# Raw inputs loaded from ScalarE's queue behind its rounding, and features-B sums in two buffers

## The chip, the cores and the metric

The kernel runs on one core of a Trainium2 chip. A core has a matmul engine (TensorE, PE in the profile; its weight loads are PEld), a vector engine (VectorE, DVE), a scalar engine (ScalarE, ACT), a general engine (GpSimd, POOL), a sync engine that here only issues DMAs (SyncE, SP), and 16 DMA engines that carry what any engine issues. Each engine works through its own instructions in order and waits on semaphores. The metric is the device time of one execution in microseconds, lower is better.

## The reference

Two stages over 8 x 4096 = 32768 tokens with 192 features:

```python
# 1: a causal convolution with 7 taps, softmax of the taps per head
w = exp(weight - max); w = w / (sum(w) + 1e-9)          # 8 heads of 24 features
out[b, s, h] = sum_k w[h, k] * x_pad[b, s + k, h]       # 6 zeros ahead of each sequence
# 2: an MLP with a squared relu
h = x @ w_in                 # 192 -> 2048
r = maximum(h, 0)
g = s * (r * r) + b
return g @ w_out             # 2048 -> 192
```

All data are float32.

## The kernel before, in words

**Tiles.** The 192 features are split into features A (the first 128) and features B (the last 64). Tokens are handled in 32 groups n of 1024, each of two blocks j of 512 tokens. The 2048 hidden features are eight pairs p of 256. Features A of a group are one raw tile `xA` (128 x 1030, with six columns of the tokens before), features B of both blocks are stacked in one raw tile `xB` (128 x 518). Both come from the pool `xin` (line 102), which has one buffer of each, so a group's raw tile can be loaded only when the convolution of the group before has read it.

**Convolution.** DVE makes it with seven instructions (taps) a piece (`Tokens.conv`, lines 180 and 182). A group has three pieces: B, A0 and A1. A piece `acc` is then split in a high and a low half for the matmuls (`Tokens.split`): ACT rounds it (L214), DVE subtracts the rounded part (L207), and two DMAs on SP copy the halves crosswise (`swap`, L190 and L191).

**A step.** For n, j, p the function `first` makes 18 matmuls into one of two PSUM tiles `h` (L527). ACT takes the relu (L555), which frees that `h`, and the square (L563). DVE rounds it (`qh`, L565) and subtracts (`ql`, L569). Two steps later `second` multiplies by the output weights for features A (12 matmuls, L700). After the eighth pair ACT evicts two accumulators (L707, L708), POOL adds them (L709) and SP stores the sum (L710).

**A batch.** The squares are kept in a ring of twelve tiles (line 97), and every 24 steps `batch` makes the features-B sums of three blocks in a row: for each block 64 small matmuls as the trace counts them (`second_B`, L719), some pieces of convolution, and `evict_B`:

```python
nc.scalar.activation(o, accs[0], AF.Identity, scale=sb, bias=bias[:, 1:2])   # L729, o is oB
nc.scalar.activation(o2, accs[1], AF.Identity, scale=sb)                     # L730, o2 is oB2
nc.gpsimd.tensor_tensor(o, o, o2, op=ALU.add)                                # L731
nc.sync.dma_start(oC, o[DB:P])                                               # L732
nc.gpsimd.tensor_tensor(oC, oC, o[0:DB], op=ALU.add)                         # L733
nc.sync.dma_start(outT[P:D, t0 : t0 + BLK], oC)                              # L734
```

The buffers oA, oB, oC, oB2 and oA2 are five parts of one tile `outs` (line 99, places in line 590), one of each.

**What sets the order.** The whole program is unrolled. `in_order` (line 944) keeps the instructions of DVE, ACT and PE in the order in which the code makes them, DMAs that one of them issues included. SP's and POOL's order behind the start is chosen by the compiler's scheduler from its own estimate of when each instruction can go. The convolution is a generator (`pieces`, line 770): `step` and `batch` draw a given number of parts from it with `convolve`. One part is one tap, one rounding, or one subtraction with its swap. A rounding is held back (`gate`) until a set step, while the taps of the next piece may run ahead. Between the last tap and the gate the code issues the next group's raw loads (lines 779 to 784): xB behind piece B, xA behind piece A1, on SP, and only ordered behind the last DMA of the start (`headed`). For every fourth group, which begins a sequence, POOL also clears the first six columns (L166). Lines 168 and 172 are the two loads.

Of the kernel before, what the change touches and what calls it, by code (L numbers as in the profile page):

```python
# [9 lines left out]
F32 = mybir.dt.float32  # L10
# [7 lines left out]
P = 128  # L18
BLK = 512
# [28 lines left out]
def conv_attention_then_squared_relu_mlp(  # L48
# [23 lines left out]
    nc = tc.nc  # L72
# [3 lines left out]
    PAD = K - 1  # L76
    DB = D - P
    NF = 2 * NPAIR
    SUP = 2 * BLK
    NSUP = T // SUP  # L80
# [15 lines left out]
    xs = ctx.enter_context(tc.tile_pool(name="xs", bufs=2))  # L96
    act = ctx.enter_context(tc.tile_pool(name="act", bufs=RING))
    wide_w = ctx.enter_context(tc.tile_pool(name="wide_w", bufs=1))
    outs = wide_w.tile([P, 5, BLK], F32, name="outs")
    W = wide_w.tile([P, NPAIR, 2, CB], F32R, name="W")  # L100
    WB = wide_w.tile([P, NPAIR, 2, DB], F32, name="WB")
    xin = ctx.enter_context(tc.tile_pool(name="xin", bufs=1))
# [5 lines left out]
    def last_of(*engines):  # L108


        traced = nc.cur_bb.bb.instructions
        last = [next(i for i in reversed(traced) if i.engine == e.engine) for e in engines]

        @contextmanager
        def context():
            with ExitStack() as stack:
                for i in last:
                    stack.enter_context(tc.issue_after(i))
                yield

        return context
# [23 lines left out]
    class Tokens:  # L145
# [3 lines left out]

        def load(self):  # L150
            n = self.n
            if n == 0:
                self.load_B()
                self.load_A(PAD + BLK)
                fetch(0, 0, CI)
                nc.sync.dma_start(self.xA[:, PAD + BLK :], xA[:, BLK:SUP])
            else:
                self.load_B()
                self.load_A(PAD + SUP)

        def load_A(self, cut):
            t0 = self.n * SUP
            self.xA = xin.tile([P, PAD + SUP], F32, name="xA")
            skip = PAD if t0 % seq == 0 else 0
            if skip:
                nc.gpsimd.memset(self.xA[:, 0:PAD], 0.0)  # L166
            x0 = t0 - PAD
            nc.sync.dma_start(self.xA[:, skip:cut], xA[:, x0 + skip : x0 + cut])

        def load_B(self):  # L170
            self.xB = xin.tile([P, PAD + BLK], F32, name="xB")
            nc.sync.dma_start(self.xB, xB[self.n])

        def conv(self, acc, x, w, width):

# [161 lines left out]
    def fetch(p, a=0, z=None):  # L337
        if a == 0:
            words[p] = places[p % 3][:, 0 : 2 * CT].rearrange("p (f w) -> p f w", w=2)
        z = z or CT  # L340
        nc.sync.dma_start(
            words[p][:, a:z].rearrange("p f w -> p (f w)"), w_words[p, :, 2 * a : 2 * z]
        )
# [19 lines left out]
    tok = {0: Tokens(0)}  # L363
# [224 lines left out]
        return w_outA(1, f, r)  # L588

    room = {"oA": 0, "oB": 1, "oC": 2, "oB2": 3, "oA2": 4}  # L590

    def out_tile(name):
        return outs[:, room[name], :]

    held = {}

# [10 lines left out]
    def second_whole(n, j, p, qh, ql):  # L607
# [17 lines left out]
        if p == NPAIR - 1:  # L625
            t0 = n * SUP + j * BLK
            oA, oB = (hold(n, j, k) for k in range(2))
            oB = oB[0:DB]
            nc.scalar.activation(oA, a1, AF.Identity, scale=sb)
            oC = out_tile("oC")[0:DB]  # L630
            nc.scalar.activation(oC, a2[DB:P, :], AF.Identity, scale=sb[DB:P])
            nc.vector.scalar_tensor_tensor(
                oB, a2[0:DB, :], sb[0:DB], oC, op0=ALU.mult, op1=ALU.add
            )
            unbiased.append((oA, outT[0:P, t0 : t0 + BLK], 0))
            unbiased.append((oB, outT[P:D, t0 : t0 + BLK], 2))
            del acc[n, j]

    def second_split(n, j, p, qh, ql):
# [19 lines left out]
        if p == NPAIR - 1:  # L659
            t0 = n * SUP + j * BLK  # L660
            early = (n, j) == (1, 0)

            o = {k: hold(n, j, k) for k in range(2)}
            for k, name in ((1, "oB"), (0, "oA")):
                o[k + 2] = out_tile(name + "2")
                nc.scalar.activation(
                    o[k], accs[k], AF.Identity, scale=sb, bias=0.0 if early else bias[:, k : k + 1]
                )
                nc.scalar.activation(o[k + 2], accs[k + 2], AF.Identity, scale=sb)
            nc.gpsimd.tensor_tensor(o[1], o[1], o[3], op=ALU.add)  # L670

            oC = out_tile("oC")[0:DB]
            nc.sync.dma_start(oC, o[1][DB:P])
            nc.gpsimd.tensor_tensor(o[0], o[0], o[2], op=ALU.add)
            toA, toB = outT[0:P, t0 : t0 + BLK], outT[P:D, t0 : t0 + BLK]
            oB = o[1][0:DB] if early else oC
            if not early:
                nc.sync.dma_start(toA, o[0])
            nc.gpsimd.tensor_tensor(oB, oC, o[1][0:DB], op=ALU.add)
            if early:  # L680
                unbiased.extend(((o[0], toA, 0), (oB, toB, 2)))
            else:
                nc.sync.dma_start(toB, oB)
            del acc[n, j]
# [81 lines left out]
    queue = []  # L766
# [3 lines left out]
    def pieces():  # L770

        def whole(n, kind, j):
            t = tok.setdefault(n, Tokens(n))
            acc = xs.tile([P, BLK], F32, name="acc")
            x = t.xB if kind == "B" else t.xA[:, j * BLK :]
            for k, _ in enumerate(t.conv(acc, x, tapB if kind == "B" else tapA, BLK)):
                if k < K - 1:
                    yield None
            with headed():
                if kind == "B" and n + 1 < NSUP:  # L780
                    tok[n + 1] = Tokens(n + 1)
                    tok[n + 1].load_B()
                elif j == 1 and n + 1 < NSUP:
                    tok[n + 1].load_A(PAD + SUP)
            yield "tapped"
            gate = 16 * n - (0 if j else 8 if kind == "A" else 16)
            while n + j > 1 and now[0] < gate:
                yield "gated"
            once = (n, kind) == (1, "B")
            split = t.split_B_at_once(acc) if once else t.split(kind, j, acc)  # L790
            next(split)
            yield "after" if once else "cast"
            next(split)
            ready.add((n, kind, j))
            yield None

        order = [(1, "A", 0), (1, "B", 0), (1, "A", 1)]
        for n in range(2, NSUP):
            order += [(n, "B", 0), (n, "A", 0), (n, "A", 1)]
        todo = [whole(*c) for c in order]  # L800
        ahead = False
        while todo:
            said = next(todo[0], "over")
            if said == "over":
                todo.pop(0)
                ahead = False
                continue
            if said in ("cast", "gated") and len(todo) > 1 and not ahead:
                if said == "cast":
                    yield said  # L810
                said = next(todo[1])
                ahead = said == "tapped"
            yield said
# [130 lines left out]
    with in_order(nc.vector, nc.scalar, nc.tensor):  # L944
        with in_order(nc.sync):
            head()
        headed = last_of(nc.sync)
# [58 lines left out]
```

## Time and profile before

| | |
|---|---|
| Median of 3 runs | 2259.8 us (2258.36 to 2260.03) |
| The profiled execution | 2259.81 us, its span 2258.0 us |
| Granted TensorE clock | 0.998 |
| Busy: PE, DVE, ACT, POOL | 99%, 71%, 59%, 12% of the span |
| DMA queue of SP (q1) | 114.50 MB, 18.3% of 16 engines |
| DMA queue of ACT (q10) | 0.13 MB, 0.0% |

The profile is of one execution. Its span runs from the first to the last instruction; the device time of the same execution is 1.8 us longer. A row of a timeline has the start in the span, the length (both in microseconds), the engine, the line of the kernel, the operation, what it writes and reads, how many instructions are merged in the row, and, in brackets, how long the engine stood idle before it and what ended that wait. A row of the waits has who waited for whom, the total, the number of times and the longest. A row for one line of code has the durations in nanoseconds (least, median, most). SPq and ACTq are the sequencers, which issue DMAs.

### The profile page before, as it was taken

How to read it: one execution, taken by the hardware profiler on the slowest of the kernel's cores; microseconds unless marked ns; L12 is line 12 of the kernel's file. 1: busy time of each engine (PE TensorE's matmuls, PEld its weight loads, DVE VectorE, ACT ScalarE, POOL GpSimd, SP SyncE). 2: the span in 40 equal slices, each digit the busy share in tenths (PEclk: the TensorE clock that was granted, in tenths of full speed). 3: DMA queues.
4: the chain of work that ended last, by engine and by line, in shares of the span. 5: the costliest groups of instructions: out<-in, count | busy, mean ns of one | idle time of the engine just before them, and what ended most of it. 6: DMA issues, size and time to landing. Idle time of an engine off the chain costs nothing.

```text
span 2258.0 us, 44538 instructions
## 1 busy us (share of the span) xinstructions
PE 2229.2 (99%) x19334; PEld 1616.9 (72%) x19334; DVE 1601.9 (71%) x1859; ACT 1323.9 (59%) x1449; POOL 274.7 (12%) x199
## 2 busy tenths in 40 slices
PE   9999999999999999999999999999999999999999
PEld 6788686868677676768686767767686858686775
DVE  8888677767776676767677767775776767677753
ACT  8758464646555464746465656556474646465654
POOL 0011101010101111110101010101111010102011
PEclk9999999999999999999999999999999999999999
DMA  5112212121211112121211211111212121112110
GB/s 164 38 37 82 62 34 62 43 52 49 55 53 53 45 45 60 41 62 39 56 38 53 57 52 48 52 55 41 59 36 62 34 62 43 53 40 59 48 36 22
DMA packets 46004, 117.48 MB, mean 52 GB/s; under 512 B 7728, under 2 KB 7984, under 8 KB 45808
## 3 DMA queue, kind: packets, MB, share of 16 engines
q1 hardware_dynamic: 45664, 114.50, 18.3%
q8 instruction: 151, 2.47, 0.5%
q14 instruction: 45, 0.37, 0.1%
q10 hardware_dynamic: 144, 0.13, 0.0%
HBM read 31.64 MB, written 25.17 MB: 25 GB/s over the span
## 4 chain that ended last, share of the span: by engine, by line
PE 77%; DVE 7%; ACT 6%; DMA 5%; POOL 3%; issue 2%; SPq 0%; DVEq 0%; POOLq 0%; ACTq 0%
PE h L527 42%; PE acc L700 27%; PE acc L719 4%; DMA outs<-outs 4%; DVE acc L182 4%; ACT q L563 2%; ACT q L555 2%; POOL outs L733 2%; DVE ql L569 2%; PE acc L646 2%; DVE qh L565 1%; ACT outs L730 1%; POOL outs L731 1%; PE h L719 1%; PE acc L256 1%
## 5 line engine op out<-in xcount | busy, mean ns | idle before, releaser
L555 ACT ACTIVATE q<-h 128x1024 f32<-128x1024 f32 x512 | 525.0, 1025 | 437.2 <-PE h L527 428.1
L565 DVE CAST qh<-q 128x1024 fp32r<-128x1024 f32 x482 | 334.9, 695 | 486.5 <-ACT q L563 484.8
L569 DVE TENSOR_TENSOR ql<-q,qh 128x1024 fp32r<-128x1024 f32 x498 | 613.9, 1233 | 55.9 <-ACT qh L565 4.9
L700 PE MATMUL acc<-qh,W 64*128 64x512 f32 x3816 | 591.6, 387 | 0.0
L563 ACT ACTIVATE q<-q 128x1024 f32<-128x1024 f32 x512 | 543.4, 1061 | 16.1
L527 PE MATMUL h<-sA,W 64*128 64x512 f32 x3024 | 431.1, 390 | 17.4 <-ACT q L555 17.4
L527 PE MATMUL h<-wB,W 64*128 64x512 f32 x1536 | 431.6, 387 | 0.0
L527 PE MATMUL h<-sB,W 64*128 64x512 f32 x1536 | 431.6, 387 | 0.0
L527 PE MATMUL h<-wA,W 64*128 64x512 f32 x3024 | 428.5, 387 | 0.6 <-DMA wA<-sA 0.6
L700 PEld LDWEIGHTS acc<-qh,W 64*128 64x128 f32 x3816 | 362.1, 184 | 73.2 <-issue 0.8
L719 PE MATMUL acc<-q,WB 64*64 64x512 f32 x3712 | 402.9, 590 | 0.0
L700 PE MATMUL acc<-ql,W 64*128 64x512 f32 x1908 | 378.6, 390 | 5.6 <-DVE ql L569 5.6
L527 PEld LDWEIGHTS h<-sA,W 64*128 64x128 f32 x3024 | 282.4, 184 | 95.4 <-ACT q L555 23.4
L182 DVE SCALAR_TENSOR_TENSOR acc<-xA,tap,acc 128x512 f32<-128x512 f32 x378 | 326.4, 864 | 6.8
L527 PEld LDWEIGHTS h<-wA,W 64*128 64x128 f32 x3024 | 286.6, 185 | 60.0 <-DMA wA<-sA 1.4
L719 PEld LDWEIGHTS acc<-q,WB 64*64 64x64 f32 x3712 | 140.0, 133 | 252.3 <-issue 252.3
L527 PEld LDWEIGHTS h<-wB,W 64*128 64x128 f32 x1536 | 283.1, 184 | 30.4
L527 PEld LDWEIGHTS h<-sB,W 64*128 64x128 f32 x1536 | 283.1, 184 | 30.2 <-issue 0.2
L709 POOL TENSOR_TENSOR outs<-outs 128x512 f32<-128x512 f32 x59 | 99.6, 1688 | 1293.8 <-ACT outs L708 1293.8
L729 ACT ACTIVATE outs<-acc,bias,sb 128x512 f32<-128x512 f32 x58 | 45.2, 779 | 325.8 <-POOL outs L733 294.5
L700 PEld LDWEIGHTS acc<-ql,W 64*128 64x128 f32 x1908 | 182.0, 184 | 53.0 <-DVE ql L569 17.6
L182 DVE SCALAR_TENSOR_TENSOR acc<-xB,tap,acc 128x512 f32<-128x512 f32 x186 | 167.0, 898 | 3.6
(145 smaller groups left out, 879.1 us busy)
## 6 DMA issues: line engine op xcount, KB each, us to landing
wA<-sA SPq DMA_DIRECT2D x124, 256.0 KB, 3.7
wB<-sB SPq DMA_DIRECT2D x62, 256.0 KB, 3.5
outT<-outs SPq DMA_DIRECT2D x59, 256.0 KB, 2.0
xA<-in_xA SPq DMA_DIRECT2D x24, 515.0 KB, 3.7
xB<-in_xB SPq DMA_DIRECT2D x32, 259.0 KB, 2.8
outT<-outs SPq DMA_DIRECT2D x62, 128.0 KB, 2.3
outs<-outs SPq DMA_DIRECT2D x59, 128.0 KB, 2.2
q<-in_w SPq DMA_DIRECT2D x7, 768.0 KB, 4.6
```

What stands on the lines that cost most here:

```text
L182: nc.vector.scalar_tensor_tensor(acc, src, w[:, k : k + 1], acc, op0=ALU.mult, op1=ALU.add)
L527: nc.tensor.matmul(h[:, i, :], w_in(w, p, chunk[0], rows), chunk[part], start=start, stop=stop)
L555: nc.scalar.activation(q, h, AF.Relu)
L563: nc.scalar.activation(q, q, AF.Square)
L565: cast(qh, q)
L569: nc.vector.tensor_tensor(ql, q, qh.bitcast(F32), op=ALU.subtract)
L646: nc.tensor.matmul(accs[to + 2 * i][0:cols], w(f, r), q[r, f % 2, :], start=start and f == 0, stop=stop and f == NF - 1,)
L700: nc.tensor.matmul(accs[i], w(f, r), q[r, f % 2, :], start=f == 0 and lo == 0, stop=f == ends[i] and lo == 2,)
L709: nc.gpsimd.tensor_tensor(o, o, o2, op=ALU.add)
L719: nc.tensor.matmul(accs[r.start // HB][i * DB : (i + 1) * DB], WB[r, p, i, :], q[r, i, :], start=p == 0, stop=p == NPAIR - 1, skip_group_c ...
L729: nc.scalar.activation(o, accs[0], AF.Identity, scale=sb, bias=bias[:, 1:2])
L733: nc.gpsimd.tensor_tensor(oC, oC, o[0:DB], op=ALU.add)
```

## The change

Three things are changed. The raw loads of groups 2 to 31 move from SP's queue to ACT's, and from behind the last tap to behind the rounding L214 of the same piece. They lose the order that `headed` gave them and stand in ACT's fixed order instead; the POOL memset of the six columns is written in the code at the new place too. The loads of groups 0 and 1 stay on SP. The sums of features B get a second buffer: `outs` has six parts, and each call for oB takes the part that the call before did not take (parts 1 and 5). That is 2 KB more for each partition.

```diff
-    outs = wide_w.tile([P, 5, BLK], F32, name="outs")
+    outs = wide_w.tile([P, 6, BLK], F32, name="outs")
...
-        def load_A(self, cut):
+        def load_A(self, queue, cut=PAD + SUP):
...
-            nc.sync.dma_start(self.xA[:, skip:cut], xA[:, x0 + skip : x0 + cut])
+            queue.dma_start(self.xA[:, skip:cut], xA[:, x0 + skip : x0 + cut])
...
-            nc.sync.dma_start(self.xB, xB[self.n])
+            queue.dma_start(self.xB, xB[self.n])
...
     room = {"oA": 0, "oB": 1, "oC": 2, "oB2": 3, "oA2": 4}
+    turn = [0]

     def out_tile(name):
-        return outs[:, room[name], :]
+        k = room[name]
+        if name == "oB":
+            turn[0] = 1 - turn[0]
+            k += 4 * turn[0]
+        return outs[:, k, :]
...
-            with headed():
-                if kind == "B" and n + 1 < NSUP:
-                    tok[n + 1] = Tokens(n + 1)
-                    tok[n + 1].load_B()
-                elif j == 1 and n + 1 < NSUP:
-                    tok[n + 1].load_A(PAD + SUP)
             yield "tapped"
             gate = 16 * n - (0 if j else 8 if kind == "A" else 16)
             while n + j > 1 and now[0] < gate:
...
             split = t.split_B_at_once(acc) if once else t.split(kind, j, acc)
             next(split)
+            if kind == "B" and n + 1 < NSUP:
+                tok[n + 1] = Tokens(n + 1)
+                tok[n + 1].load_B(nc.scalar)
+            elif j == 1 and n + 1 < NSUP:
+                tok[n + 1].load_A(nc.scalar)
             yield "after" if once else "cast"
```

More of the change, by code (lines that the diff above doesn't have):

```diff
@@ L151, in load @@
             n = self.n
-            if n == 0:
-                self.load_B()
-                self.load_A(PAD + BLK)
+            self.load_B(nc.sync)
+            if n:
+                self.load_A(nc.sync)
+            else:
+                self.load_A(nc.sync, PAD + BLK)
                 fetch(0, 0, CI)
                 nc.sync.dma_start(self.xA[:, PAD + BLK :], xA[:, BLK:SUP])
-            else:
-                self.load_B()
-                self.load_A(PAD + SUP)
-        def load_A(self, cut):
+        def load_A(self, queue, cut=PAD + SUP):
             t0 = self.n * SUP
@@ L167, in load_A, with load_B @@
             x0 = t0 - PAD
-            nc.sync.dma_start(self.xA[:, skip:cut], xA[:, x0 + skip : x0 + cut])
-        def load_B(self):
+            queue.dma_start(self.xA[:, skip:cut], xA[:, x0 + skip : x0 + cut])
+        def load_B(self, queue):
             self.xB = xin.tile([P, PAD + BLK], F32, name="xB")
-            nc.sync.dma_start(self.xB, xB[self.n])
+            queue.dma_start(self.xB, xB[self.n])
         def conv(self, acc, x, w, width):
```

## The prediction

> **What bounds the kernel now.** I read the busy table first, then the waits of the matmul engine (PE), then the timelines of each engine around the places where PE stood still. The busy table says that PE is the engine to follow:
>
> ```profile
> PE 2229.2 (99%) x19334; PEld 1616.9 (72%) x19334; DVE 1601.9 (71%) x1859; ACT 1323.9 (59%) x1449; POOL 274.7 (12%) x199
> ```
>
> So nothing counts that does not close a hole in PE. The waits of PE (total us, times, longest) name nearly all of its holes:
>
> ```profile
> PE h L527 <- ACT q L555: 17.4, 10, 2.2
> PE acc L700 <- DVE ql L569: 5.6, 16, 0.4
> ...
> PE h L527 <- DMA wA<-sA: 0.6, 1, 0.6
> ```
>
> The 26 of the first two rows all lie just behind a batch, the stretch in which PE makes the features-B sums of three blocks (L719). Nineteen batches come 24 steps apart; the one at 2134 comes when the last raw input has long been loaded. Its PE timeline is the measure for the others (start, length):
>
> ```profile
> 246.31 1.95 PE L719 MATMUL acc<-q,WB 64*64 64x512 f32 x16
> ...
> 2130.59 0.84 PE L527 MATMUL h<-sA,W 64*128 64x512 f32 x6
> ...
> 2134.08 0.66 PE L719 MATMUL acc<-q,WB 64*64 64x512 f32 x4
> ...
> 2154.84 0.98 PE L527 MATMUL h<-sA,W 64*128 64x512 f32 x6
> ...
> 2158.42 0.84 PE L527 MATMUL h<-sA,W 64*128 64x512 f32 x6
> ...
> 2161.82 0.84 PE L527 MATMUL h<-sA,W 64*128 64x512 f32 x6
> ```
>
> A step without a stall is 2161.82 - 2158.42 = 3.40 us. A batch is 2154.84 - 2134.08 = 20.76, the step behind it 3.58, the step before it 3.49. Between two batches lie 24 steps, so a period without loss is 20.76 + 3.58 + 22 x 3.40 + 3.49 = 102.63 us. The first batch starts at 246.31 and the nineteenth at 2134.08: 18 periods took 1887.77 us instead of 1847.3. **PE loses 40.4 us there**, 2.2 a period. That is more than the 23 us of waits, since a matmul that restarts also follows at a wider distance.
>
> Batches alternate between two kinds. In the first kind both waits of PE are seen (batch at 1504):
>
> ```profile
> 1524.98 0.98 PE L527 MATMUL h<-sA,W 64*128 64x512 f32 x6
> ...
> 1528.56 0.84 PE L527 MATMUL h<-sA,W 64*128 64x512 f32 x6
> ...
> 1534.27 0.96 PE L527 MATMUL h<-sA,W 64*128 64x512 f32 x6 [2.15 <-ACT q L555]
> ...
> 1538.46 0.85 PE L527 MATMUL h<-sA,W 64*128 64x512 f32 x6
> ...
> 1542.10 0.85 PE L527 MATMUL h<-sA,W 64*128 64x512 f32 x6
> ```
>
> Against 3.40 the last three steps shown take 5.71, 4.19 and 3.64: 3.34 us lost, 2.31 of it in the first. ScalarE (ACT) shows why:
>
> ```profile
> 1511.36 0.78 ACT L729 ACTIVATE outs<-acc,bias,sb 128x512 f32<-128x512 f32 x1 [0.49 <-PE acc L719]
> 1512.03 0.68 ACT L730 ACTIVATE outs<-acc,sb 128x512 f32<-128x512 f32 x1
> 1524.98 0.78 ACT L729 ACTIVATE outs<-acc,bias,sb 128x512 f32<-128x512 f32 x1 [12.26 <-POOL outs L733]
> ...
> 1531.95 0.78 ACT L729 ACTIVATE outs<-acc,bias,sb 128x512 f32<-128x512 f32 x1 [5.62 <-POOL outs L733]
> ...
> 1533.20 1.02 ACT L555 ACTIVATE q<-h 128x1024 f32<-128x1024 f32 x1
> ```
>
> The second and third evictions want to write the one buffer oB, which POOL's last add of the block before (L733) still reads; the relu (L555) that gives PE its next h buffer stands behind them. L733 in turn waits for the copy L732, and SP could not issue that:
>
> ```profile
> 1519.06 0.34 SPq L168 DMA_DIRECT2D xA<-in_xA  x1
> 1519.49 0.46 SPq L732 DMA_DIRECT2D outs<-outs  x1
> ```
>
> POOL and VectorE (DVE) say what each of the two had waited for:
>
> ```profile
> 1512.86 1.68 POOL L731 TENSOR_TENSOR outs<-outs 128x512 f32<-128x512 f32 x1 [5.77 <-ACT outs L730]
> ...
> 1523.68 1.26 POOL L733 TENSOR_TENSOR outs<-outs 64x512 f32<-64x512 f32 x1 [9.14 <-DMA outs<-outs]
> ```
>
> ```profile
> 1513.33 5.70 DVE L182 SCALAR_TENSOR_TENSOR acc<-xA,tap,acc 128x512 f32<-128x512 f32 x6
> ```
>
> The copy's data stood from 1512.86 + 1.68 = 1514.54. The raw load L168 is ahead of it in SP's order and waits for the last tap at 1519.03. The copy is 4.9 us late for a load that nobody needs yet.
>
> In the second kind (batch at 1400) an xB load does the same, with a shorter delay; PE then only lacks the low halves:
>
> ```profile
> 1414.23 0.34 SPq L172 DMA_DIRECT2D xB<-in_xB  x1
> 1414.67 0.47 SPq L732 DMA_DIRECT2D outs<-outs  x1
> ```
>
> ```profile
> 1421.28 0.98 PE L527 MATMUL h<-sA,W 64*128 64x512 f32 x6
> ...
> 1431.45 0.50 PE L700 MATMUL acc<-ql,W 64*128 64x512 f32 x2 [0.34 <-DVE ql L569]
> ```
>
> ```profile
> 1427.22 1.02 ACT L555 ACTIVATE q<-h 128x1024 f32<-128x1024 f32 x1
> ```
>
> The batch at 2134 has one oB buffer too, but no load ahead of the copy:
>
> ```profile
> 2150.04 0.78 ACT L729 ACTIVATE outs<-acc,bias,sb 128x512 f32<-128x512 f32 x1 [7.47 <-POOL outs L733]
> ...
> 2157.75 1.02 ACT L555 ACTIVATE q<-h 128x1024 f32<-128x1024 f32 x1
> ```
>
> Counted from the first h behind the batch, the relu starts 1533.20 - 1524.98 = 8.2 us late in the first kind, 1427.22 - 1421.28 = 5.9 in the second and 2157.75 - 2154.84 = 2.9 here, where nothing is lost. So the bound in this stage is the time of that relu: 2.9 costs nothing, 5.9 costs the low-half stall, 8.2 costs both.
>
> **The change, part by part.** *The copy is freed.* No load stands ahead of L732 on SP, so it goes as in the batch at 2134. There L733 was done, and let the second eviction go, at 2150.04, 15.96 us after the batch's start. The batch at 1504 starts at 1524.98 - 20.76 = 1504.22, so its first L733 is done near 1520.2 instead of 1524.9.
>
> *Two buffers.* The second eviction writes the other oB and needs only its sum. The three sums are ready 6.92 us apart (20.76 / 3), at about 1511.1, 1518.1 and 1525.0. The second goes at 1518.3; the third, which shares its oB with the first, finds it free since 1520.2 and goes at 1525.2. With its partner it takes 0.78 + 0.68, to about 1526.6. The relu then waits for h alone: 2.5 us behind the first h, earlier than the harmless 2.9. The low halves follow it by about 4.2 us (relu, square, cast, subtraction), so the 16 waits on ql go too. What is late next is nothing on PE; oC stays single, but POOL and SP alone wait for it, and oB2 is free when L731 is done, some 4 us ahead of each next use. The larger outs moves the tiles behind it by 2 KB a partition. No row shows such a shift; it could only lengthen or shorten instructions off PE's way, with the cover that the next part finds.
>
> *The loads on ACT.* Sixty loads (two for each of 30 groups) leave SP and stand on ACT directly behind the rounding L214. What they wait for, DVE's last tap, the rounding has already waited for, so no new wait is added; the cost is the issue. The trace has one DMA issued by ACT, and SP's own for the same load, with its time to landing:
>
> ```profile
> L764 ACTq DMA_DIRECT2D outT<-outs x1: 371/371/371, 2254.6 to 2254.6; - x1
> ```
>
> ```profile
> L168 SPq DMA_DIRECT2D xA<-in_xA x32: 333/346/431, 1.7 to 2090.1; - x32
> ...
> DMA to landing us min/median/max: 3.4/3.7/5.7
> ```
>
> So about 0.37 us each, 22 us of ACT in all. Queued behind are the next relu and square, and through them DVE's cast and PE. By the order that the code sets, which repeats every 48 steps with six loads, four of six fall into ordinary steps. Such a step on ACT, DVE and PE:
>
> ```profile
> 1553.19 0.60 ACT L214 CAST sA<-acc 128x512 fp32r<-128x512 f32 x1
> 1554.56 1.03 ACT L555 ACTIVATE q<-h 128x1024 f32<-128x1024 f32 x1 [0.77 <-PE h L527]
> ```
>
> ```profile
> 1557.51 1.23 DVE L569 TENSOR_TENSOR ql<-q,qh 128x1024 fp32r<-128x1024 f32 x1
> ...
> 1565.46 0.48 DVE L180 TENSOR_SCALAR acc<-xA,tap 128x512 f32<-128x512 f32 x1
> ```
>
> ```profile
> 1561.61 0.39 PE L700 MATMUL acc<-ql,W 64*128 64x512 f32 x2
> ```
>
> ACT idles 0.77 us behind the rounding, which hides 0.37. Were it not enough, the low half is ready at 1558.74 and used at 1561.61, 2.87 us later. So a load may hold ACT for 0.77 + 2.87 = 3.64 us before PE notices. Between an issue of 0.37 and one that lasts to the landing, 5.7 at most, I take the first, the only row of ACT itself, and so a price of nothing. The other two loads fall behind roundings inside or just ahead of a batch, where PE has 20.76 us of its own work.
>
> *Later loads.* They now wait for the rounding, which the code holds back to a set step. The tightest is the xA load behind the rounding at 1553.19: its first reader is the L180 at 1565.46, 11.7 us after the rounding ends, against a landing of 3.7, at most 5.7. Hidden by 6 us or more. The memset of the first columns moves on POOL with the load and only waits less.
>
> *Sum.* Of the 40.4 us I leave 2 (the wait for a swap, third row of the waits above, and some 0.08 a batch): 38.4 us go. The profiled execution took 2259.81 us with a span of 2258.0; the median of the three runs is 2259.8, so one scale serves both. 2259.8 - 38.4 = 2221.4 us.
>
> **The rivals.** *Only half of it:* the relu's stall goes, but the low halves stay late, because DVE, SP's new order or the third eviction still holds the relu to about 5 us. For it: the batch at 1400 shows the ql stall without any PE wait on ACT. Against it: at 2.9 us it is gone, and I find 2.5. What goes are ten waits of 1.74 on average, each with 0.16 of wider spacing (2.31 - 2.15): 19.0 us. Time 2241.
>
> *No change:* the queue is not what matters, and the loads only move their issue. Sixty times 0.35 us, 21 us, leave SP, none of it on PE's way: 2259.8. Beside this stands the Trainium skill, "DMA: Bandwidth & Descriptors", section "Issuing engines are not separate DMA queues": issuing from several engines saves only the time on the sequencer that it takes to initiate the DMA, usually small. By that rule as it stands the time would be 2259.8. Here the copy was late by the 4.9 us in which the load stood first in SP's order, waiting, and that speaks against the rule as a full account.
>
> *Slower:* a load holds ACT until some transfer in flight on SP's queue has landed, for instance over a shared completion count. Its place are the 40 loads in ordinary steps; beyond 3.64 us each further microsecond costs PE 40 us. It decides from 3.64 + 38.4 / 40 = 4.6 us a load. Held for the longest landing above, with the issue, 0.35 + 5.7 = 6.05, that is 40 x 2.41 = 96 us lost and 38.4 won: 2317. At the median landing, 4.05, it would be 16 lost: 2238, still faster. Against it: SP itself issued L732 0.43 us after L168, without awaiting its landing.
>
> **How the numbers follow.** A measurement of this kernel can tell about 0.2% (4.5 us) from no change. The forecast has 0.77, half of it 0.14, no change 0.04, slower 0.05. The likeliest time is 2221.4. If all 40.4 us go it is 2219.4; the lower end, 2217, adds some 2 us for the steps ahead of the first batch, which the periods don't count. The upper end takes in the half case, 2241. Faster by over 0.2% is 0.77 + 0.14 = 0.91, within 0.2% 0.04, slower 0.05.
>
> **What would show it.** Right: L729 waits for PE's sums and no longer for L733; L732 follows L731 within some tenths; the relu starts about 2.5 us behind the first h; the two waits of PE shrink to near nothing; batches stand 102.7 us apart. Wrong: ACT idle behind a DMA issue, L180 waiting for xA or xB, or ql waits that remain behind the batches.

## The result, and the profile after

The changed kernel takes 2220.59 us (median of four runs, 2220.06 to 2221.55); the kernel before, beside it, 2259.91 us. The ratio is 0.983 (95% interval 0.981 to 0.984). Faster was forecast, with 2221.4 us.

The change moves the lines: L729, L731, L732 and L733 of before are now L733, L735, L736 and L737; L527, L555 and L719 are L526, L554 and L723. First the busy table of the page and the waits of PE:

```profile
PE 2213.0 (100%) x19334; PEld 1617.7 (73%) x19334; DVE 1638.0 (74%) x1859; ACT 1329.0 (60%) x1449; POOL 287.1 (13%) x199
```

```profile
PE acc L391 <- POOL xA L165: 1.0, 1, 1.0
PE h L526 <- DMA wA<-sA: 0.3, 1, 0.3
PE acc L620 <- DVE ql L568: 0.2, 1, 0.2
```

The 26 waits behind the batches (17.4 and 5.6 us) are gone; what is left is a single wait for a swap and two near the start. PE's timeline has the first and the nineteenth batch:

```profile
246.00 1.52 PE L723 MATMUL acc<-q,WB 64*64 64x512 f32 x12
...
2094.80 2.38 PE L723 MATMUL acc<-q,WB 64*64 64x512 f32 x20
```

18 periods now take 1848.8 us, 102.71 each; without loss they would take 1847.3. The loss of 40.4 us has become 1.5. The 18 periods are shorter by 1887.77 - 1848.80 = 39.0 us, of the 39.5 us by which the span became shorter (2258.0 to 2218.5).

The batch that was at 1504 is now at 1478.6. ACT, POOL and SP in it ("issue" stands for time in which the engine waited for nothing that the profile shows):

```profile
1492.57 0.78 ACT L733 ACTIVATE outs<-acc,bias,sb 128x512 f32<-128x512 f32 x1 [5.51 <-PE acc L723]
...
1499.49 0.78 ACT L733 ACTIVATE outs<-acc,bias,sb 128x512 f32<-128x512 f32 x1 [5.56 <-issue]
...
1501.74 1.03 ACT L554 ACTIVATE q<-h 128x1024 f32<-128x1024 f32 x1 [0.90 <-PE h L526]
```

```profile
1487.14 1.75 POOL L735 TENSOR_TENSOR outs<-outs 128x512 f32<-128x512 f32 x1 [5.70 <-ACT outs L734]
1492.63 1.27 POOL L737 TENSOR_TENSOR outs<-outs 64x512 f32<-64x512 f32 x1 [3.75 <-DMA outs<-outs]
```

```profile
1489.02 0.54 SPq L736 DMA_DIRECT2D outs<-outs  x1
```

The batch's first copy goes 0.13 us after its data are ready (1487.14 + 1.75 = 1488.89); it was 4.9 us late. The two later copies of this batch go 0.6 and 1.0 us after theirs, since the one buffer oC is still being stored (39 of the 59 copies wait for such a store); only SP and POOL wait for that. The second eviction waits for PE's sum and goes 1.3 us ahead of the end of L737. The relu L554 waits for nothing but h. The matmuls of PE that begin a step:

```profile
1499.33 0.98 PE L526 MATMUL h<-sA,W 64*128 64x512 f32 x6
...
1502.91 0.84 PE L526 MATMUL h<-sA,W 64*128 64x512 f32 x6
...
1506.31 0.84 PE L526 MATMUL h<-sA,W 64*128 64x512 f32 x6
```

The relu starts 2.4 us behind the first h, and the steps are 3.58 and 3.40, where before they were 3.58 and 5.71.

### The profile page after: what moved, and what is told of

The parts are those of the page before. It is cut to its first block, busy times and chain, and to the rows that moved or that the text cites. A ratio compares the mean times of both kernels' runs of the same rounds, so it can differ in the third digit from the quotient of the medians.

```text
span 2218.5 us, 44403 instructions
## 1 busy us (share of the span) xinstructions
PE 2213.0 (100%) x19334; PEld 1617.7 (73%) x19334; DVE 1638.0 (74%) x1859; ACT 1329.0 (60%) x1449; POOL 287.1 (13%) x199
## 4 chain that ended last, share of the span: by engine, by line
PE 98%; DVE 1%; DMA 0%; ACT 0%; issue 0%; SPq 0%; DVEq 0%; ACTq 0%
PE h L526 47%; PE acc L704 29%; PE acc L723 18%; PE acc L650 2%; PE h L723 1%; PE acc L620 0%; PE acc L626 0%; DVE acc L181 0%; PE acc L628 0%; PE acc L627 0%; DVE ql L568 0%; DMA wA<-sA 0%; PE acc L619 0%; PE acc L622 0%; DMA xA<-in_xA 0%; DVE q L306 0%
## 5 line engine op out<-in xcount | busy, mean ns | idle before, releaser
L554 ACT ACTIVATE q<-h 128x1024 f32<-128x1024 f32 x512 | 525.6, 1026 | 493.9 <-PE h L526 485.2
L526 PE MATMUL h<-wB,W 64*128 64x512 f32 x1536 | 430.4, 387 | 0.0
L526 PE MATMUL h<-sB,W 64*128 64x512 f32 x1536 | 430.4, 387 | 0.0
L526 PE MATMUL h<-sA,W 64*128 64x512 f32 x3024 | 428.4, 388 | 0.0
L526 PE MATMUL h<-wA,W 64*128 64x512 f32 x3024 | 426.9, 387 | 0.3 <-DMA wA<-sA 0.3
L723 PE MATMUL acc<-q,WB 64*64 64x512 f32 x3712 | 402.9, 590 | 0.0
L526 PEld LDWEIGHTS h<-sA,W 64*128 64x128 f32 x3024 | 283.4, 184 | 72.7 <-issue 15.4
L181 DVE SCALAR_TENSOR_TENSOR acc<-xA,tap,acc 128x512 f32<-128x512 f32 x378 | 328.7, 870 | 6.8
L526 PEld LDWEIGHTS h<-wA,W 64*128 64x128 f32 x3024 | 285.5, 184 | 59.2 <-DMA wA<-sA 1.1
L723 PEld LDWEIGHTS acc<-q,WB 64*64 64x64 f32 x3712 | 140.0, 133 | 252.3 <-issue 252.0
L526 PEld LDWEIGHTS h<-wB,W 64*128 64x128 f32 x1536 | 283.1, 184 | 30.4
L526 PEld LDWEIGHTS h<-sB,W 64*128 64x128 f32 x1536 | 283.1, 184 | 29.6 <-issue 0.2
L181 DVE SCALAR_TENSOR_TENSOR acc<-xB,tap,acc 128x512 f32<-128x512 f32 x186 | 185.7, 998 | 3.6
L733 ACT ACTIVATE outs<-acc,bias,sb 128x512 f32<-128x512 f32 x58 | 45.1, 778 | 224.7 <-PE acc L723 139.8
```

The costliest lines, as they stand in the source:

```text
L181: nc.vector.scalar_tensor_tensor(acc, src, w[:, k : k + 1], acc, op0=ALU.mult, op1=ALU.add)
L526: nc.tensor.matmul(h[:, i, :], w_in(w, p, chunk[0], rows), chunk[part], start=start, stop=stop)
L554: nc.scalar.activation(q, h, AF.Relu)
L723: nc.tensor.matmul(accs[r.start // HB][i * DB : (i + 1) * DB], WB[r, p, i, :], q[r, i, :], start=p == 0, stop=p == NPAIR - 1, skip_group_c ...
```

## The experiments

**Theory.** The relu behind a batch sets what PE loses: it is late because each eviction waits for L733 of the block before, and that for a copy behind a waiting load. Up to some 3 us behind the first h it costs nothing. **Rivals:** both parts of the change are needed, each half; the later place of the loads is the cure and not the queue; ACT's new work is itself near PE's path. Ratios below are against the kernel before of the same series; it took 2255.0 to 2255.2 us there, 5 us less than beside the change, while the kernels without the stall took 2220.5 to 2221.1 there, as the change did. So the 5 us seem to lie in the stall itself. The one trace of that series with the stall of the kernel before, e3's, agrees: its 18 periods took 1881.6 us, 34.3 us lost instead of 40.4. In it, and in e1's, the nine copies behind a waiting xA load landed 3.6 to 3.9 us after their issue, in the trace of before 3.9 to 4.2. Why they landed earlier is open.

**The second buffer alone (e1_two_sums).** The kernel before with

```diff
-    outs = wide_w.tile([P, 5, BLK], F32, name="outs")
+    outs = wide_w.tile([P, 6, BLK], F32, name="outs")
...
+        if name == "oB":
+            turn[0] = 1 - turn[0]
+            k += 4 * turn[0]
```

> The kernel before with the second buffer for oB alone; the loads stay on SP behind the last tap. Theory (the relu behind the batch is late only because each eviction waits for L733 of the block before; 2.9 us behind the first h costs nothing): SP still issues the copy late, in the first kind of batch at 1519.5 as before, so the first L733 is done at 1524.9 and POOL's next L731 at 1526.2; but the second eviction goes at PE's sum (1518.3) and the third finds its buffer free at 1524.9, its sum at 1525.0. The relu starts 2.5 to 2.7 us behind the first h and PE loses nothing: 2221 to 2224 us. Rival (the load ahead of the copy is the cause, a second buffer only shifts the wait to oB2 and oC): at most half of the gain, 2240 us or more.

Measured: 2221.12 us, ratio 0.985 (0.983 to 0.986), as the theory had it. PE, ACT, SP and POOL in the batch at 1478.9 (copy L738, last add L739; the relu is still L555):

```profile
1499.65 0.98 PE L527 MATMUL h<-sA,W 64*128 64x512 f32 x6
```

```profile
1502.06 1.03 ACT L555 ACTIVATE q<-h 128x1024 f32<-128x1024 f32 x1 [0.90 <-PE h L527]
```

```profile
1493.72 0.34 SPq L168 DMA_DIRECT2D xA<-in_xA  x1
1494.16 0.46 SPq L738 DMA_DIRECT2D outs<-outs  x1
```

```profile
1497.90 1.26 POOL L739 TENSOR_TENSOR outs<-outs 64x512 f32<-64x512 f32 x1 [8.70 <-DMA outs<-outs]
```

The copy is still behind the load, and L739 waits 8.70 us. ACT does not notice: the relu starts 1502.06 - 1499.65 = 2.4 us behind the first h, in all nineteen batches, and PE has no wait behind any. The whole gain is there without moving a load.

**The loads alone (e2_loads_act).** The changed kernel with those lines taken back, so that oB is one buffer again.

> The changed kernel with one buffer for oB; the loads stand on ACT behind the rounding. Theory: each block still waits for L733 of the one before, but the copy goes at once, as in the batch at 2134 of the kernel before, so the relu starts about 2.9 us behind the first h in all batches and PE loses nothing: 2220 to 2224 us; the two parts of the change do the same work twice. Rival (both parts are needed, each half): about 2240 us.

Measured: 2220.46 us, ratio 0.985 (0.983 to 0.986). ACT and PE in the batch at 1478.9:

```profile
1501.17 0.78 ACT L730 ACTIVATE outs<-acc,bias,sb 128x512 f32<-128x512 f32 x1 [5.57 <-POOL outs L734]
...
1502.41 1.03 ACT L554 ACTIVATE q<-h 128x1024 f32<-128x1024 f32 x1
```

```profile
1499.64 0.98 PE L526 MATMUL h<-sA,W 64*128 64x512 f32 x6
...
1503.21 0.84 PE L526 MATMUL h<-sA,W 64*128 64x512 f32 x6
...
1506.61 0.84 PE L526 MATMUL h<-sA,W 64*128 64x512 f32 x6
```

The evictions still wait for the last add of the block before, but that comes in time: the relu starts 2.8 us behind the first h here and no step is longer than 3.58. The 2.9 us that were expected of all batches are not what came: it is 2.4 to 4.1 us, and no batch has a wait of PE behind it. So either part alone brings all of it, and the parts do not add up. The rival of two halves is out.

**The loads at the new place, on SP (e3_loads_sp_late).** As e2, with the queue put back:

```diff
-                tok[n + 1].load_B(nc.scalar)
+                tok[n + 1].load_B(nc.sync)
...
-                tok[n + 1].load_A(nc.scalar)
+                tok[n + 1].load_A(nc.sync)
```

> One buffer for oB, and the loads written at the new place behind the rounding, but issued by SP. The compiler's scheduler orders SP by its own estimate, and in this program it still puts the load ahead of the first copy of each batch, as before. Theory (what counts is that no waiting load stands ahead of the copy; ACT's fixed order is what brings that about): no change, 2258 to 2261 us, with L733 as late as before. Rival (the later place in the code is the cure): 2221 to 2225 us.

Measured: 2254.53 us, ratio 0.9998 (0.9988 to 1.0008). That is no change, as expected; it lies below the expected 2258 us because the kernel before too takes 5 us less in this series. SP, POOL and PE in the batch at 1500:

```profile
1514.69 0.35 SPq L167 DMA_DIRECT2D xA<-in_xA  x1
1515.13 0.46 SPq L733 DMA_DIRECT2D outs<-outs  x1
```

```profile
1519.05 1.26 POOL L734 TENSOR_TENSOR outs<-outs 64x512 f32<-64x512 f32 x1 [8.87 <-DMA outs<-outs]
```

```profile
1529.14 0.96 PE L526 MATMUL h<-sA,W 64*128 64x512 f32 x6 [1.36 <-ACT q L554]
```

The scheduler puts the load ahead of the copy all the same, the last add of the first block (L734) waits 8.87 us, and nothing is won. The later place in the code is no cure. This kernel and e2 differ by the queue alone, so what cures there is that the load no longer stands in SP's order ahead of the copy. An order on SP itself with the copy first was not run.

**The loads on ACT at the old place (e4_act_early).** The changed kernel with the five lines of the loads moved from behind `next(split)` to ahead of `yield "tapped"`, so that ACT itself waits for the last tap.

> The changed kernel with the loads on ACT at the old place, behind the last tap and ahead of the gate, so that ACT itself has to wait for DVE's last tap. In an ordinary step the tap ends about 1.6 us after ACT would start the next relu. Theory (an ordinary step hides 0.77 + 2.87 us of delay on ACT): the relu is late by some 2 us, PE does not notice, 2220 to 2226 us. Rival (ACT waiting for DVE costs PE directly): about 40 loads of 2 us each, 2290 to 2310 us.

Measured: 2229.64 us, ratio 0.989 (0.987 to 0.990), 4 us above the expected range and far below the rival's. ACT ahead of the first batch and in an ordinary step, and PE ahead of the first batch:

```profile
185.16 0.33 ACTq L171 DMA_DIRECT2D xB<-in_xB  x1
185.55 0.72 ACT L513 ACTIVATE q<-q,bias 128x512 f32<-128x512 f32 x1 [5.02 <-DVE acc L181]
...
1443.65 0.33 ACTq L167 DMA_DIRECT2D xA<-in_xA  x1
1444.03 1.03 ACT L554 ACTIVATE q<-h 128x1024 f32<-128x1024 f32 x1 [3.13 <-DVE acc L181]
```

```profile
187.23 0.96 PE L526 MATMUL h<-sA,W 64*128 64x512 f32 x6 [1.74 <-ACT q L554]
```

The relu at 1444.03 follows that at 1438.77 by 5.26 us instead of 3.40, so it is 1.9 us late, as expected, and PE's steps stay 3.40; over the 18 periods PE loses only 2.9 us, 1.4 more than the changed kernel. The rest is lost ahead of the first batch, which begins at 254.0 instead of 246.0. There DVE makes two taps a step, and the wait of 5.02 us on ACT alone costs PE 3.0 us (steps of 5.30 and 4.48). It is longer than the cover of 3.64 us that was read from an ordinary step; e5 below shows that the cover is also smaller there.

**ACT held behind each load (e5_hold4, e6_hold8).** The changed kernel with, behind the loads, four or eight times

```diff
+            if kind == "B" or j == 1:
+                for _ in range(4):
+                    nc.scalar.copy((t.sB if kind == "B" else t.sA[j])[:, 0, :], acc)
```

> The changed kernel, with the rounding repeated four times on ACT behind each of the 60 loads (the same result again), some 0.6 us each. A load and these hold ACT for 0.37 + 2.4 = 2.8 us. Theory (an ordinary step hides 3.64 us): PE does not notice in the ordinary steps; only the five loads before the first batch, where DVE is denser, may cost some us. 2220 to 2228 us. Rival (each delay of ACT beyond its idle 0.77 us goes to PE): 40 loads of 2 us, about 2300 us.

> The same with eight repeats: 0.37 + 4.8 = 5.2 us on ACT for each load. Theory: 1.5 us beyond the 3.64 that a step hides, at 40 loads, 62 us, and up to 10 more before the first batch: 2275 to 2295 us. Rival (the cover is much larger, ACT is not near PE's path at all): below 2235 us.

Measured: 2237.48 us (0.992, 0.991 to 0.994) and 2402.95 us (1.065, 1.064 to 1.067). Both are above what was expected, e5 by 9 us and e6 by over 100. The granted clock of e6 is 0.983, but its undisturbed steps are 3.40 us as elsewhere, so that is not where the time goes. A single load with eight repeats, ACT and PE of e6:

```profile
460.82 5.19 ACT L797 CAST sA<-acc 128x512 fp32r<-128x512 f32 x8
465.92 1.02 ACT L554 ACTIVATE q<-h 128x1024 f32<-128x1024 f32 x1
```

```profile
462.72 0.84 PE L526 MATMUL h<-sA,W 64*128 64x512 f32 x6
...
466.99 0.98 PE L526 MATMUL h<-sA,W 64*128 64x512 f32 x6 [0.71 <-ACT q L554]
...
471.17 0.85 PE L526 MATMUL h<-sA,W 64*128 64x512 f32 x6
...
474.81 0.85 PE L526 MATMUL h<-sA,W 64*128 64x512 f32 x6
```

Steps of 4.27, 4.18 and 3.64 lose 1.9 us, near the 1.5 expected. So the size for one load in an ordinary step is nearly right. But the loads are not alone. ACT and PE of e5, where two stand two steps apart with an eviction (L711, L712) between:

```profile
301.46 2.58 ACT L797 CAST sA<-acc 128x512 fp32r<-128x512 f32 x4
...
309.86 2.58 ACT L797 CAST sB<-acc 128x512 fp32r<-128x512 f32 x4
312.35 1.02 ACT L554 ACTIVATE q<-h 128x1024 f32<-128x1024 f32 x1
```

```profile
316.57 0.50 PE L704 MATMUL acc<-ql,W 64*128 64x512 f32 x2 [0.34 <-DVE ql L568]
```

ACT has no idle time from 301.46 to 312.35, so the second hold starts where the first has not been caught up, and PE misses ql. In e6 such a pair makes steps of 4.27, 4.18, 6.81 and 5.14, which is 6.8 us lost, and the holds in and ahead of a batch, which I had counted as free, make its relu 6.6 us late at most. Ahead of the first batch e5 loses 9 us and e6 28: in e5 the hold of 2.58 us at 189.6 makes PE steps of 4.17 and 4.18 there, 1.55 us lost, though it is shorter than 3.64. Holds that follow each other closely share one cover; they don't each have their own.

**The relu alone made late (e7_relu4, e8_relu8).** The changed kernel, the third eviction of each batch with four or eight more of its second instruction:

```diff
-        nc.scalar.activation(o2, accs[1], AF.Identity, scale=sb)
+        for _ in range(1 + again):
+            nc.scalar.activation(o2, accs[1], AF.Identity, scale=sb)
```

> The changed kernel, with the second instruction of the third eviction of each batch repeated four times (the same result again), which only puts the relu behind the batch later by about 2.7 us: some 4.2 us behind the first h. Theory (PE needs the end of that relu for its third h, 6.98 us behind the first, and its low halves some 4 us later): nothing is lost, 2219 to 2223 us. Rival (PE follows the relu one to one from 2.9 us on): 19 batches of 1.3 us, 2245 us.

> The same with eight repeats: the relu starts some 6.9 us behind the first h, between the 5.9 and the 8.2 of the kernel before. Theory: the third h waits about 1 us for it and the low halves cost another 1.0 as before, 19 batches of 2 us: 2255 to 2265 us, near the kernel before, with two buffers and no load on SP. Rival (the stall came from the adds and copies, not from the relu): 2220 to 2224 us.

Measured: 2220.54 us (0.985, 0.983 to 0.986) and 2264.24 us (1.004, 1.003 to 1.006), both inside the ranges of the theory. ACT and PE of e7, then of e8:

```profile
1504.12 1.02 ACT L554 ACTIVATE q<-h 128x1024 f32<-128x1024 f32 x1
```

```profile
1499.82 0.98 PE L526 MATMUL h<-sA,W 64*128 64x512 f32 x6
```

```profile
1527.83 6.46 ACT L735 ACTIVATE outs<-acc,sb 128x512 f32<-128x512 f32 x9
1534.19 1.01 ACT L554 ACTIVATE q<-h 128x1024 f32<-128x1024 f32 x1
```

```profile
1526.99 0.98 PE L526 MATMUL h<-sA,W 64*128 64x512 f32 x6
...
1535.26 0.98 PE L526 MATMUL h<-sA,W 64*128 64x512 f32 x6 [1.12 <-ACT q L554]
...
1538.41 0.49 PE L704 MATMUL acc<-ql,W 64*128 64x512 f32 x2 [0.32 <-DVE ql L568]
```

In e8, with two buffers and no load on SP, both waits of PE are back in every batch, for the relu is 1534.19 - 1526.99 = 7.2 us behind the first h. In e7 it is 1504.12 - 1499.82 = 4.3 us behind in every batch, and nothing is lost. So the time of this relu is the cause, whatever makes it late, and the point from which it costs lies between 4.3 and the 5.7 to 6.0 of the second kind of batch before.

## Why the prediction was right

**The place and the size of the loss.** The periods of PE gave 40.4 us; 39.0 came back against 38.4 in the sum. The remainder that was left standing, 2 us, measured 1.5. One reading was too tidy: the two kinds of batch do not alternate to the end. Those at 1714, 1819 and 1925 are all of the first kind, the one at 1819 behind an xB load whose copy landed only after 5.0 us. The sum went by the periods and does not need it.

**The relu as the bound.** Forecast 2.5 us behind the first h, measured 2.4; e7 and e8 show that it alone decides. The value 2.9 that was read off the batch at 2134 was a safe one and not the limit.

**The copy and the buffers.** The copy follows its data by 0.13 us, and the first L737 ends at 1493.9, 15.3 us after the start of the batch, where 15.96 was taken from the batch at 2134. What the prediction did not say: each part alone brings the whole gain (e1, e2). Its working held both facts, 2.9 us with one buffer and free sums with two, and set them in one chain instead of asking whether either would do. So the time by itself was no test of the chain: with one of its two links broken it would have come out the same.

**The loads on ACT.** Taken at 0.37 us of ACT each, hidden by 0.77. They cost ACT's engine nothing:

```profile
1523.21 1.06 ACT L562 ACTIVATE q<-q 128x1024 f32<-128x1024 f32 x1
1523.30 0.34 ACTq L167 DMA_DIRECT2D xA<-in_xA  x1
1524.17 0.60 ACT L213 CAST sA<-acc 128x512 fp32r<-128x512 f32 x1
1525.55 1.03 ACT L554 ACTIVATE q<-h 128x1024 f32<-128x1024 f32 x1 [0.77 <-PE h L526]
```

The idle time behind the rounding is still 0.77. The cover of 3.64 us fits a single load in an ordinary step, where e6 lost 1.9 us for the 1.5 expected. As forty independent covers it is wrong (e5, e6), and ahead of the first batch it is too large (e5). The slower rival was priced on it, at 96 us for 6.05 us a load; e6, with holds of 5.2 us, lost some 180. It did not come about: no load waited on ACT.

**The later loads.** The one that was named as the tightest, now issued at 1523.30, is first read by the tap at 1536.45 in DVE's timeline (no load has less than 12.9 us); the line of the xA loads has the landings:

```profile
1536.45 0.48 DVE L179 TENSOR_SCALAR acc<-xA,tap 128x512 f32<-128x512 f32 x1
```

```profile
L167 ACTq DMA_DIRECT2D xA<-in_xA x30: 334/334/335, 103.6 to 2064.1; - x30
...
DMA to landing us min/median/max: 3.2/3.6/5.6
```

13.2 us against 5.6 at most, hidden as forecast.

**The rivals.** Half of the gain would have left waits on ql; there is none behind a batch. No change and slower fell with the time.

**The rule on issuing engines.** The Trainium skill says in "DMA: Bandwidth & Descriptors", section "Issuing engines are not separate DMA queues", that only the time to initiate is saved. For how long a transfer takes, the trace agrees: 3.6 us to landing on ACT's queue, 3.7 on SP's. As an account of what a change of queue can bring it fell: e2 and e3 differ by the queue alone, and by 34 us, because on SP the scheduler's order sets the waiting load ahead of the copy, which must wait with it.

## What to carry to other kernels

A DMA that waits on a sequencer delays the DMAs behind it, here by 4.9 us; look in the queue's timeline for a load that is issued the moment its buffer comes free, and for what goes out just after it. Before adding up the parts of a change, ask of each whether it alone takes the wait off the path: here two cures met the same chain and the second is worth nothing. A cover read from one quiet step is good for one delay, and two delays within the time that it takes to catch up share it.

## What the runs showed of the hardware

**A DMA on ACT can be issued ahead of the arithmetic before it.** In the code the load stands behind the rounding; in the trace above it goes at 1523.30, while the square runs and 0.87 us before the rounding starts. This issue, whose buffer was free, cost ACT nothing. A wait does: in e4 ACT stood 3.13 us behind a load that waited for DVE.

**DVE's taps are longer beside POOL's adds.** The rows of the convolution's taps on features B (L182 before, L181 after), busy time in microseconds and mean in nanoseconds, first of before and then of the change:

```profile
L182 DVE SCALAR_TENSOR_TENSOR acc<-xB,tap,acc 128x512 f32<-128x512 f32 x186 | 167.0, 898 | 3.6
```

```profile
L181 DVE SCALAR_TENSOR_TENSOR acc<-xB,tap,acc 128x512 f32<-128x512 f32 x186 | 185.7, 998 | 3.6
```

The instructions are the same, 100 ns longer on average; the taps on xA gained only 6 ns (864 to 870). The overlaps in the two traces bear out the cause. Of the 564 instructions of this kind on xB and xA, those with no POOL add beside them took 0.74 to 0.76 us in both traces, without exception; the others, 95 before and 129 after, took 1.5 us on average. Now that the copies go at once, POOL's adds fall among the taps: in the batch at 1478.6 the six taps of A1 take 6.78 us where they took 5.70. The Trainium skill, "SBUF — State Buffer", section "SBUF: two separate sides", says that such an instruction of DVE, with two SBUF inputs, and a GpSimd instruction that reads SBUF exclude each other; the longer taps agree. It cost PE nothing here: in that batch DVE still waits 3.19 us for ACT's next square.

**A copy lands later right behind another transfer.** In the trace of the change, 40 of the 59 copies L736 have no other DMA ahead of them that is still under way, and land 2.2 us after their issue in the median. Ten, issued 0.7 to 2 us behind a swap, take 3.5 (3.0 to 4.3). In the trace of before, nine that are issued 0.44 us behind an xA load take 4.0 (3.9 to 4.2), and nine that are issued 0.4 to 0.7 us behind an xB load, half as many bytes, 3.1 (2.8 to 5.0). So the load made the copy of the batch at 1504 wait 4.9 us and land later besides; the freed copy of that batch, now behind a swap, lands after 3.5.
